# Softcap attention with two gated layers on one core: third key tile's scores in plain fp32, its sums partly on VectorE

## Chip, core and metric

The kernel runs on one core of a Trainium2 chip. The metric is the device time of one execution in microseconds; lower is better. Three runs of the kernel before gave 323.43, 324.13 and 324.26 us, the median is 324.13 us.

## What is computed

Attention over 2 batches, 12 heads, 448 positions and 64 channels per head, with scores capped by a tanh, then a gated layer with spatial mixing, then a gated layer with a convolution over positions. All in fp32. Cut to what the change touches:

```python
scale = 1.0 / np.sqrt(q.shape[-1])
scores = scale * np.matmul(q, k.transpose(0, 1, 3, 2))
scores = cap * np.tanh(scores / cap)
scores = scores - np.max(scores, axis=-1, keepdims=True)
attn = np.exp(scores)
attn = attn / (np.sum(attn, axis=-1, keepdims=True) + 1e-09)
out = np.matmul(attn, v)
...
h = gelu(x @ w_in)          # x: the heads side by side, 768 wide; h: 1024 wide
# then normalisation, a 448 x 448 mix, w_out; then x @ w2_in, a convolution, a gate, w2_out
```

## The kernel before

The heads go in pairs: 12 pairs `N` (6 per batch), the two heads of a pair on SBUF partitions 0 to 63 and 64 to 127. Scores are computed transposed, keys on PSUM partitions and the 448 queries along the free axis, in key tiles of 128, 128, 128 and 64 keys. The exponentials need no maximum, since the cap bounds them.

Two halves of a pair are two steps `R = 2 * N + half` of the loop at L619. `scores(N, 0)` computes key tiles 0 and 1 of both heads into the PSUM tile `sc` (one buffer), ScalarE takes a tanh (L412) and an exponential (L421) of it into `raw`. `scores(N, 1)` does the same for tile 2 (128 keys) and the last 64 keys. A product in full fp32 accuracy is made in one of two ways. In the first, VectorE splits an operand into a rounded `fp32r` part and a remainder, and TensorE runs three fp32r matmuls (high by high, high by low, low by high); key tiles 0 to 2 go this way, with `prep_q` and `prep_k` making the splits, `prep_q` for the next pair, with the factor `qscale = 1 / (8 * cap)` put on it. In the second, TensorE multiplies plain fp32 operands, which the trace shows as two records per matmul; the last 64 keys go this way, as four matmuls of 64 x 64 weights, one per quarter of the array, from `klast` (the keys times `qscale`) and the raw queries `qr`.

The sum over the keys and the product with the values are TensorE work as well. `value(N, g)` multiplies key tile g of `raw` by the values `V` (plain fp32, four column groups of 32 side by side), into the PSUM tile `pv`. For the softmax's denominator, VectorE adds tile 0 and tile 1 of `raw` into `held` (the tile `sm`, L472), and `values` multiplies it by a block of ones (`su`, four matmuls); after the second half, eight more such matmuls sum key tile 2 and the last keys. `norm` then copies sums and products out of PSUM (`E`, L542, ScalarE), sends the sums through DRAM to spread them over partitions (`ss`, `d`, `rb`, GpSimd's queue), and VectorE multiplies and splits the result into `X`, the input of the next stage. The last pair does this on TensorE instead (`norm_pe`, with the matmuls `pv<-E,sel`).

Beside this, the weights of the next stage are read (`f`, one piece of 128 x 512 float64 words at the steps in `WIN`), and turned into fp32r pairs `WI` by `decode_half`: `hd` (a cast), a shift and an or into `f`, a cast to `WI`, and a subtraction for the remainder, the last three on VectorE, the first on VectorE in the early pairs and on ScalarE from `R = 11` on. `FILL` puts pieces of the next stage's first products (`mo`, `fi`) between the attention's matmuls at the steps R = 15, 19, 23 and after the last scores at 24, 25 and 26.

Two things set the order. TensorE's attention matmuls go through `ordered`, which chains each to the one before, so they stand in the order of the code. `pin` chains instructions of ScalarE, VectorE and the SP queue in the same way where it is used; the rest is placed by the compiler's scheduler, which estimates times and issues what it takes to be ready. On the chip every engine then works through its fixed list.

`values(N, ...)` lags behind `scores`: on TensorE, the values and sums of pair N - 1 stand between the scores of pair N. A round, in what follows, is the stretch from the first score matmul of a pair to that of the next pair.

Of the kernel before, what the change touches and what calls it, by code (L numbers as in the profile page):

```python
# [19 lines left out]
P = 128  # L20
# [18 lines left out]
TAKEN = 4  # L39

# [13 lines left out]
def stages(  # L54
# [228 lines left out]
    def attention(att, psa):  # L283
# [5 lines left out]
        Kt = [att.tile([P, 2, ST], F32R, name=f"K{i}") for i in range(2)]  # L289
        kraw = [att.tile([P, S], F32, name=f"kr{i}") for i in range(2)]  # L290
        klast = [att.tile([P, D], F32, name=f"kl{i}") for i in range(2)]
        qraw = {}

        def load(n):
            b, p = divmod(n, NPAIR)
            qr = att.tile([P, S], F32, tag="qr", name="qr", bufs=3)
            kr = kraw[n % 2]
            k0 = 0 if n else K0
            for h in range(2):
                r = slice(h * D, (h + 1) * D)  # L300
                dma = sync if n or h else nc.scalar.dma_start
                dma(qr[r], qT[b, p, r, h])
                if k0:
# [15 lines left out]
        def prep_q(n):  # L319
            qr, _ = qraw[n]  # L320
            q = Qt[n] = att.tile([P, 2, S], F32R, tag="Q", name="Q", bufs=2)
            if n == 0:

                lasta[0] = A.activation(q[:, 0], qr, AF.Copy)
                lastv[0] = V.tensor_tensor(out=q[:, 1], in0=qr, in1=f(q[:, 0]), op=ALU.subtract)
                return
            V.tensor_scalar(out=q[:, 0], in0=qr, scalar1=qscale[:, 0:1], scalar2=None, op0=ALU.mult)
            lastv[0] = V.scalar_tensor_tensor(
                out=q[:, 1], in0=qr, scalar=qscale[:, 0:1], in1=f(q[:, 0]),
                op0=ALU.mult, op1=ALU.subtract,  # L330
            )

        def prep_k(n, c=slice(0, ST)):
            _, kr = qraw[n]
            K = Kt[n % 2]
            lastv[0] = split(kr[:, c], K[:, 0, c], K[:, 1, c])
            if c.stop < ST:
                return
            if n == 0:
                G.tensor_copy(klast[0], kr[:, ST:])  # L340
            else:
                V.tensor_scalar(
                    out=klast[n % 2], in0=kr[:, ST:], scalar1=qscale[:, 0:1], scalar2=None, op0=ALU.mult
                )
# [24 lines left out]
        with pin(lastv):  # L369
            prep_k(0, slice(0, K0))  # L370
        constants(att)
        creg = A.alloc_register("creg")
        with pin(lasta):
            A.reg_load(creg, capc[0:1].bitcast(mybir.dt.int32))

# [9 lines left out]
        with pin(lastv):  # L385
            prep_k(0, slice(K0, ST))
# [14 lines left out]
        def scores(N, half, then=None):  # L401
# [6 lines left out]
            sc = {"scale": qscale} if N == 0 else {}  # L408

            def soft(x, ps):  # L410
                with pin(lasta):
                    lasta[0] = A.activation(x, ps, AF.Tanh, **sc)  # L412
                if N == 1 and half:
                    with pin(lasta):
                        late.pop()()
                if half or N:
                    expo(x)
# [12 lines left out]
            for g in range(2 * half, 2 * half + 2):  # L430
# [4 lines left out]
                if g < 3:  # L435

                    for i, (j, l) in enumerate(((0, 0), (0, 1), (1, 0))):
                        for h in range(2):
                            r = slice(h * D, (h + 1) * D)
                            out, x = to[:, g * 2 + h, :S] if g < 2 else ps[:, h, :2], q[r, l]  # L440
                            if g == 2:
                                x = x.rearrange("p (i c) -> p i c", i=2)
                            ordered(out, lhsT=K[r, j, c], rhs=x, start=i == 0, stop=i == 2)
                else:

                    qr, _ = qraw.pop(N)
                    for h in range(2):
                        r = slice(h * D, (h + 1) * D)
                        for i in range(2):
                            ordered(  # L450
                                ps[i * D : (i + 1) * D, h, 2], lhsT=klast[N % 2][r],
# [14 lines left out]
            if half:  # L466
                soft(raw, ps)
            elif N:
# [31 lines left out]
        def values(N, half, done=False):  # L500
# [11 lines left out]
            for g in range(2 * half, 3 * half + 1):  # L512
                x = raw if half else held.pop(N)
                for t in range(4):
# [4 lines left out]
                        rhs=x[:, h, g - 2 + c if g == 2 else 2] if half else x[:, h, c * HS : (c + 1) * HS],  # L519
# [99 lines left out]
        for R in range(2 * NN + LAGS[1] + 1):  # L619
# [40 lines left out]
            if R in FILL:  # L660

                i, k0, k1 = FILL[R]
                if k0 == 0:
                    if i == 1:
                        free = psa.tile([P, 4, 512], F32, tag="sc", name="fi", bufs=1)
                    fill[i] = free[:, i, :S] if i % 2 else psm.tile([P, 512], F32, tag="mo", name="mo")[:, :S]
# [84 lines left out]
    def rest():  # L751
# [183 lines left out]
        with ExitStack() as s2, ExitStack() as last:  # L935
# [40 lines left out]
            def f_unit(b, m):  # L976
# [128 lines left out]
```

## Time and profile before

| | |
|---|---|
| median of three runs | 324.13 us |
| the profiled execution | 323.95 us |
| its span, first to last instruction | 322.1 us |
| TensorE busy in the span | 314.3 us (98%) |
| VectorE busy | 227.1 us (70%) |
| ScalarE busy | 207.0 us (64%) |
| attention | from the start to about 107 us of the span |

The profile is of one execution. A page gives the busy time of each engine and the chain of work that ended last; the timeline gives each engine's instructions in order of time, with the idle time before an instruction and what ended it in brackets. Starts of matmuls are good measures, their ends are modelled: how long a group of matmuls takes is read from its start to the start of the next group. Plain fp32 matmuls count twice in the timeline (x8 for four).

### The profile page before, as it was taken

What the parts mean: (1) busy time and instruction counts of PE and PEld (TensorE: products, weight loads), DVE (VectorE), ACT (ScalarE), POOL (GpSimd) and SP (SyncE); (2) the same over time, 40 slices, a digit from 0 to 9 for tenths busy, and PEclk for the clock granted to TensorE, in tenths of its full rate; (3) what the DMA queues carried; (4) which work ended last, traced back from release to release, by engine and by line L of the source; (5) the groups of instructions that cost most, each with busy time, mean ns of one, the idle gap of its engine ahead of it and who ended that gap; (6) DMA issues with size and microseconds to landing.
All of it is one profiled execution on the core that took longest, in us unless ns stands there. A gap on an engine that the chain in (4) does not pass through costs nothing.

```text
span 322.1 us, 6326 instructions
## 1 busy us (share of the span) xinstructions
PE 314.3 (98%) x2374; PEld 260.2 (81%) x2374; DVE 227.1 (70%) x474; ACT 207.0 (64%) x342; POOL 41.1 (13%) x76
## 2 busy tenths in 40 slices
PE   8999999999999999999999999999999999999992
PEld 6566666666677789988999999999999999999992
DVE  4557797699485999879995999979999997000000
ACT  4999999898963466646854745568867986111010
POOL 4000132241342060211112000000000000000000
PEclk9999999999999999999999999999999999999998
DMA  3477996855432253132124570012592301110111
GB/s 113 122 216 200 261 246 150 242 159 170 147 121 88 71 162 94 59 98 67 35 98 164 198 259 0 3 65 67 156 319 79 98 3 58 57 59 28 57 58 38
DMA packets 24526, 37.72 MB, mean 117 GB/s; under 512 B 7608, under 2 KB 22472, under 8 KB 24488
## 3 DMA queue, kind: packets, MB, share of 16 engines
q1 hardware_dynamic: 22552, 34.22, 34.3%
q0 software_dynamic: 1632, 2.61, 3.1%
q8 instruction: 20, 0.33, 0.4%
q10 hardware_dynamic: 304, 0.41, 0.4%
q14 instruction: 18, 0.15, 0.2%
HBM read 34.39 MB, written 2.79 MB: 115 GB/s over the span
## 4 chain that ended last, share of the span: by engine, by line
PE 95%; SPq 2%; DMA 1%; issue 0%; DVE 0%; ACT 0%; ACTq 0%
PE mo L114 18%; PE mo L112 18%; PE mo L113 18%; PE pv L395 16%; PE sc L395 9%; PE mo L798 3%; PE mo L799 3%; PE mo L800 3%; PE mo L395 3%; PE fi L395 2%; SPq L86 2%; DMA V<-in_vL_dram 1%; PE mo L845 1%; PE mo L844 1%; PE idle L395 0%
## 5 line engine op out<-in xcount | busy, mean ns | idle before, releaser
L112 PE MATMUL mo<-X,WI 128*128 128x448 f32 x120 | 43.5, 365 | 0.0
L114 PE MATMUL mo<-X,WI 128*128 128x448 f32 x120 | 43.5, 365 | 0.0
L113 PE MATMUL mo<-X,WI 128*128 128x448 f32 x120 | 43.5, 365 | 0.0
L421 ACT ACTIVATE raw<-raw 128x1344 f32<-128x1344 f32 (+2 forms) x25 | 36.4, 1461 | 0.7
L114 PE MATMUL mo<-HG,W 128*128 128x448 f32 x96 | 35.1, 365 | 0.0
L113 PE MATMUL mo<-HG,W 128*128 128x448 f32 x96 | 35.0, 365 | 0.0
L112 PE MATMUL mo<-HG,W 128*128 128x448 f32 x96 | 34.4, 365 | 0.0
L412 ACT ACTIVATE raw<-sc 128x1792 f32<-128x1792 f32 (+1 forms) x22 | 32.5, 1476 | 2.2 <-PE sc L395 2.0
L395 PE MATMUL pv<-raw,V 128*32 128x224 f32 x576 | 32.9, 358 | 0.2 <-DMA V<-in_vL_dram 0.2
L986 DVE TENSOR_SCALAR o<-mo 128x224 f32<-128x224 f32 x1 | 0.4, 392 | 44.8 <-ACT o L985 44.8
L989 ACT ACTIVATE o<-mo 128x448 f32<-128x448 f32 x11 | 5.8, 538 | 35.8 <-PE mo L114 35.8
L395 PEld LDWEIGHTS pv<-raw,V 128*32 128x32 f32 x576 | 19.0, 109 | 11.6 <-issue 5.8
L395 PE MATMUL sc<-Q,K 64*128 64x448 f32 x210 | 27.6, 385 | 0.5 <-ACT raw L412 0.4
L395 PEld LDWEIGHTS sc<-Q,K 64*128 64x128 f32 x210 | 17.9, 184 | 9.7 <-ACT raw L412 5.6
L112 PEld LDWEIGHTS mo<-X,WI 128*128 128x128 f32 x120 | 22.5, 188 | 1.9
L113 PEld LDWEIGHTS mo<-X,WI 128*128 128x128 f32 x120 | 22.5, 188 | 1.9
L114 PEld LDWEIGHTS mo<-X,WI 128*128 128x128 f32 x120 | 22.5, 188 | 1.9
L153 ACT ACTIVATE hs<-f 128x256 f16<-128x256 bf16 x36 | 16.4, 487 | 6.3 <-DMA f<-in_w_in_dram 6.0
L112 PEld LDWEIGHTS mo<-HG,W 128*128 128x128 f32 x96 | 18.0, 188 | 1.4
L114 PEld LDWEIGHTS mo<-HG,W 128*128 128x128 f32 x96 | 18.0, 188 | 1.4
L113 PEld LDWEIGHTS mo<-HG,W 128*128 128x128 f32 x96 | 18.0, 188 | 1.4
L168 DVE TENSOR_TENSOR WI<-f,WI 128x256 fp32r<-128x256 f32 (+1 forms) x36 | 18.2, 510 | 0.9 <-ACT WI L163 0.7
(159 smaller groups left out, 702.4 us busy)
## 6 DMA issues: line engine op xcount, KB each, us to landing
f<-in_w_out_dram SPq DMA_DIRECT2D x36, 255.8 KB, 2.7
f<-in_w_in_dram SPq DMA_DIRECT2D x12, 511.8 KB, 5.0
f<-in_w_in_dram SPq DMA_DIRECT2D x24, 255.8 KB, 3.3
qr<-in_qT_dram SPq DMA_DIRECT2D x23, 112.0 KB, 3.5
rb<-d POOLq DMA_DIRECT2D x22, 112.0 KB, 3.6
out_dram<-o SPq DMA_DIRECT2D x11, 224.0 KB, 1.9
V<-in_vL_dram SPq DMA_DIRECT2D x12, 192.0 KB, 4.0
kr<-in_kT_dram SPq DMA_DIRECT2D x11, 112.0 KB, 3.7
```

What stands on the lines that cost most here:

```text
L86: lasts[0] = nc.sync.dma_start(dst, src)
L112: matmul(ps, lhsT=whi, rhs=xhi, start=start, stop=False)
L113: matmul(ps, lhsT=whi, rhs=xlo, start=False, stop=False)
L114: matmul(ps, lhsT=wlo, rhs=xhi, start=False, stop=stop)
L153: A.activation(half, top, AF.Copy)
L168: V.tensor_tensor(out=lo, in0=f(low), in1=f(hi), op=ALU.subtract)
L395: lastm[0] = T.matmul(*args, **kw)
L412: lasta[0] = A.activation(x, ps, AF.Tanh, **sc)
L421: lasta[0] = A.activation(x, x, AF.Exp, scale=creg)
L798: T.matmul(ps, lhsT=xs(0, k), rhs=WI[1][:, 0, k], start=k == 0, stop=False)
L799: T.matmul(ps, lhsT=xs(0, k), rhs=WI[1][:, 1, k], start=False, stop=False)
L800: T.matmul(ps, lhsT=xs(1, k), rhs=WI[1][:, 0, k], start=False, stop=k == NK - 1)
```

## The change

1. Key tile 2 is no longer split. Its scores are plain fp32 in quarters, four matmuls of 64 keys by 64 channels with 448 columns each, from the raw keys and the raw queries, in place of six fp32r matmuls. `prep_k` splits 256 keys in place of 384, and `klast` is gone: the last 64 keys are read from `kr` as well, which gets three rotating buffers in place of two fixed ones.
2. The factor `qscale` moves from the operands to the tanh, as its scale (a register `qreg` on ScalarE; the first pair had it there already). `prep_q` becomes a plain split.
3. In the seven pairs of `ADD`, VectorE adds key tile 2 of `raw` into `held` after the second half's exponential. Those pairs have no sum matmuls after the first half; after the second, four matmuls sum `held` and four the last keys.
4. The fills at R = 15, 19 and 23 stand after the sums in place of before the values; at R = 24, both halves of the last pair's values come together, ahead of the fill of R = 25.
5. The last output tile is taken out of PSUM by one ScalarE instruction in place of one on ScalarE and one on VectorE.

```diff
+ADD = (1, 2, 3, 5, 7, 9, 10)
...
-            kr = kraw[n % 2]
+            kr = att.tile([P, S], F32, tag="kr", name="kr", bufs=3)
...
-            V.tensor_scalar(out=q[:, 0], in0=qr, scalar1=qscale[:, 0:1], scalar2=None, op0=ALU.mult)
-            lastv[0] = V.scalar_tensor_tensor(
-                out=q[:, 1], in0=qr, scalar=qscale[:, 0:1], in1=f(q[:, 0]),
-                op0=ALU.mult, op1=ALU.subtract,
-            )
+            lastv[0] = split(qr, q[:, 0], q[:, 1])
...
-            lastv[0] = split(kr[:, c], K[:, 0, c], K[:, 1, c])
...
+            lastv[0] = split(kr[:, :K0], K[:, 0], K[:, 1])
...
+            A.reg_load(qreg, qscale[0:1].bitcast(mybir.dt.int32))
...
-            sc = {"scale": qscale} if N == 0 else {}
+            sc = qreg if N else qscale
...
-                    lasta[0] = A.activation(x, ps, AF.Tanh, **sc)
+                    lasta[0] = A.activation(x, ps, AF.Tanh, scale=sc)
...
+                elif g == 2:
+                    qr, kr = qraw[N]
+                    x = qr.rearrange("p (i c) -> p i c", i=2)
+                    for h in range(2):
+                        r = slice(h * D, (h + 1) * D)
+                        for i in range(2):
+                            o, w = slice(i * D, (i + 1) * D), slice(K0 + i * D, K0 + (i + 1) * D)
+                            ordered(ps[o, h, :2], lhsT=kr[r, w], rhs=x[r], start=True, stop=True)
...
                 soft(raw, ps)
+                if N in ADD:
+                    x = held[N].rearrange("p h (i c) -> p h i c", i=2)
+                    V.tensor_tensor(out=x, in0=x, in1=raw[:, :, :2], op=ALU.add)
...
-            for g in range(2 * half, 3 * half + 1):
-                x = raw if half else held.pop(N)
+            for g in ((0, 3) if half else ()) if N in ADD else ((2, 3) if half else (0,)):
+                x = raw if g else held.pop(N)
...
+            if R in FILL and R >= 2 * NN:
+                units()
             tick()
             if R > 2 and done < 2 * NN and R - done >= LAGS[R >= LAGS[2]]:
                 values(*divmod(done, 2))
                 done += 1
+                if R == 2 * NN:
+                    values(*divmod(done, 2))
+                    done += 1
+            if R in FILL and R < 2 * NN:
+                units()
...
-                    A.activation(o[:, :HS], ps[:, :HS], AF.Copy, scale=0.5)
-                    V.tensor_scalar(out=o[:, HS:], in0=ps[:, HS:], scalar1=0.5, scalar2=None, op0=ALU.mult)
+                    A.activation(o, ps, AF.Copy, scale=0.5)
```

The order of VectorE around rounds 2 and 3, before. `sm_258` belongs to pair 1, `sm_336` to pair 2, `Q_338` and `K1` to pair 3, `f64_282` is the first piece of weights:

```order
L472 TENSOR_TENSOR sm_258<-raw_239 128x896
L327 TENSOR_SCALAR Q_338<-qr_230,one_72 128x448
L106 CAST K1_88<-kr1_90 128x384
L342 TENSOR_SCALAR kl1_92<-kr1_90,one_72 128x64
L328 SCALAR_TENSOR_TENSOR Q_338<-qr_230,one_72,Q_338 128x448
L109 TENSOR_TENSOR K1_88<-kr1_90,K1_88 128x384
L155 CAST hd0_137<-f64_282 128x512
L159 SCALAR_TENSOR_TENSOR f64_282<-f64_282,hd0_137 128x512
L165 CAST WI0_76<-f64_282 128x512
L168 TENSOR_TENSOR WI0_76<-f64_282,WI0_76 128x512
L472 TENSOR_TENSOR sm_336<-raw_321 128x896
```

The same place of VectorE's list after the change. `sm_253` belongs to pair 1, `raw_279` is that pair's second half, `sm_330` belongs to pair 2:

```order
L467 TENSOR_TENSOR sm_253<-raw_234 128x896
L108 CAST Q_332<-qr_224 128x448
L108 CAST K1_88<-kr_225 128x256
L111 TENSOR_TENSOR Q_332<-qr_224,Q_332 128x448
L111 TENSOR_TENSOR K1_88<-kr_225,K1_88 128x256
L157 CAST hd0_135<-f64_276 128x512
L161 SCALAR_TENSOR_TENSOR f64_276<-f64_276,hd0_135 128x512
L167 CAST WI0_76<-f64_276 128x512
L170 TENSOR_TENSOR WI0_76<-f64_276,WI0_76 128x512
L462 TENSOR_TENSOR sm_253<-sm_253,raw_279 128x896
L467 TENSOR_TENSOR sm_330<-raw_315 128x896
```

The new addition (L462) of pair 1 stands behind the four instructions of the first piece of weights, where pair 2's `sm` stood; pair 2's follows it. The additions of pairs 2 and 3 stand in the same way behind the second and third piece.

TensorE in round 2, before. `pv` rows with `raw_285`, `sm_258` are pair 1's, `sc` rows pair 2's:

```order
L395 MATMUL sc_320<-Q_276,K0_87 128x448 x12
L395 MATMUL pv_161<-raw_239,V_168 32x224 x16
L395 MATMUL pv_161<-sm_258,ones2_145 32x224 x4
L395 MATMUL sc_366<-Q_276,K0_87 128x2x224 x6
L395 MATMUL sc_366<-qr_162,kl0_91 64x224 x4
L395 MATMUL pv_161<-raw_285,vlast_110 64x224 x4
L395 MATMUL pv_161<-raw_285,V_168 32x224 x8
L395 MATMUL pv_161<-raw_285,ones2_145 32x224 x4
L395 MATMUL pv_161<-raw_285,ones0_143 32x224
```

And after the change:

```order
L382 MATMUL sc_314<-Q_271,K0_87 128x448 x12
L382 MATMUL pv_157<-raw_234,V_165 32x224 x16
L382 MATMUL sc_355<-qr_158,kr_159 64x2x224 x4
L382 MATMUL sc_355<-qr_158,kr_159 64x224 x4
L382 MATMUL pv_157<-raw_279,vlast_108 64x224 x4
L382 MATMUL pv_157<-raw_279,V_165 32x224 x8
L382 MATMUL pv_157<-sm_253,ones2_144 32x224 x4
L382 MATMUL pv_157<-raw_279,ones0_142 32x224
```

The sum over `sm` of pair 1 moved from ahead of the second half's scores to the end of the round, and now reads what VectorE's new addition wrote; the second half's scores follow the first values at once.

TensorE where the scores have ended, before:

```order
L395 MATMUL fi_1326<-X_75,WI0_76 128x448 x18
L395 MATMUL pv_161<-raw_1223,V_1118 32x224 x16
L395 MATMUL pv_161<-sm_1238,ones2_145 32x224 x4
L395 MATMUL mo_1382<-X_75,WI0_76 128x448 x18
L395 MATMUL pv_161<-raw_1269,vlast_110 64x224 x4
L395 MATMUL pv_161<-raw_1269,V_1118 32x224 x8
L395 MATMUL pv_161<-raw_1269,ones2_145 32x224 x4
```

And after the change, where the fill of R = 23 (`mo`, x6) comes just ahead:

```order
L382 MATMUL mo_872<-X_75,WI0_76 128x448 x6
L382 MATMUL fi_1274<-X_75,WI0_76 128x448 x18
L382 MATMUL pv_157<-raw_1179,V_1080 32x224 x16
L382 MATMUL pv_157<-sm_1194,ones2_144 32x224 x4
L382 MATMUL pv_157<-raw_1221,vlast_108 64x224 x4
L382 MATMUL pv_157<-raw_1221,V_1080 32x224 x8
L382 MATMUL pv_157<-raw_1221,ones2_144 32x224 x4
```

The last pair's values and sums are one group there, with the 18 `mo` matmuls behind it.

## Rows read from the trace of the kernel before

**Rows 1.** The page: the span, and the chain that ended last, by engine.

```profile
span 322.1 us, 6326 instructions
...
PE 95%; SPq 2%; DMA 1%; issue 0%; DVE 0%; ACT 0%; ACTq 0%
```

**Rows 2.** Timeline of TensorE, round 2: start us, us, engine, instruction.

```profile
17.89 1.49 PE L395 MATMUL sc<-Q,K 64*128 64x448 f32 x12
19.31 1.76 PE L395 MATMUL pv<-raw,V 128*32 128x224 f32 x32
20.85 0.60 PE L395 MATMUL pv<-sm,ones 128*32 128x224 f32 x8
21.37 0.88 PE L395 MATMUL sc<-Q,K 64*128 64x448 f32 x6
22.18 0.61 PE L395 MATMUL sc<-qr,kl 64*64 64x224 f32 x8
22.61 0.56 PE L395 MATMUL pv<-raw,vlast 64*64 64x224 f32 x8
23.10 0.98 PE L395 MATMUL pv<-raw,V 128*32 128x224 f32 x16
23.88 0.96 PE L395 MATMUL pv<-raw,ones 128*32 128x224 f32 x16
24.77 1.49 PE L395 MATMUL sc<-Q,K 64*128 64x448 f32 x12
```

**Rows 3.** Timeline of ScalarE, rounds 2, 3 and 8.

```profile
18.33 1.33 ACT L421 ACTIVATE raw<-raw 128x1344 f32<-128x1344 f32 x1
19.55 1.67 ACT L412 ACTIVATE raw<-sc 128x1792 f32<-128x1792 f32 x1
...
26.29 1.67 ACT L412 ACTIVATE raw<-sc 128x1792 f32<-128x1792 f32 x1 [0.16 <-PE sc L395]
...
68.99 0.79 ACT L153 ACTIVATE hd<-f 128x512 f16<-128x512 bf16 x1
```

**Rows 4.** Timeline of VectorE, rounds 2 to 5; in brackets idle time, and its releaser.

```profile
23.20 0.52 DVE L155 CAST hd<-f 128x512 f16<-128x512 bf16 x1 [2.15 <-DMA f<-in_w_in_dram]
...
25.77 1.08 DVE L472 TENSOR_TENSOR sm<-raw 128x896 f32<-128x896 f32 x1
...
30.32 0.51 DVE L155 CAST hd<-f 128x512 f16<-128x512 bf16 x1 [1.59 <-DMA f<-in_w_in_dram]
...
32.82 1.08 DVE L472 TENSOR_TENSOR sm<-raw 128x896 f32<-128x896 f32 x1
...
37.84 0.54 DVE L155 CAST hd<-f 128x512 f16<-128x512 bf16 x1 [1.93 <-DMA f<-in_w_in_dram]
...
40.27 1.08 DVE L472 TENSOR_TENSOR sm<-raw 128x896 f32<-128x896 f32 x1
```

**Rows 5.** Timeline of the SP queue: the issue of the first piece of weights.

```profile
18.71 0.43 SPq L86 DMA_DIRECT2D f<-in_w_in_dram  x1
```

**Rows 6.** Timeline of TensorE, round 7, the fill of R = 15.

```profile
56.70 0.61 PE L395 MATMUL sc<-qr,kl 64*64 64x224 f32 x8
57.24 1.48 PE L395 MATMUL mo<-X,WI 128*128 128x448 f32 x6
58.65 0.61 PE L395 MATMUL pv<-raw,vlast 64*64 64x224 f32 x8
```

**Rows 7.** Timeline of ScalarE and VectorE, the last output tiles.

```profile
306.64 0.54 ACT L989 ACTIVATE o<-mo 128x448 f32<-128x448 f32 x1 [4.32 <-PE mo L114]
...
316.37 0.36 ACT L985 ACTIVATE o<-mo 128x224 f32<-128x224 f32 x1 [4.32 <-PE mo L114]
...
316.75 0.39 DVE L986 TENSOR_SCALAR o<-mo 128x224 f32<-128x224 f32 x1 [44.85 <-ACT o L985]
```

**Rows 8.** Windows at the span's end: us, busy by engine, granted clock, DMA.

```profile
318.00:320.00 2.00, 0.00 (x0) 0.00 (x0) 0.00 (x0) 0.00 (x0) 0.00 (x0) 0.91 0.35 123
320.00:322.00 2.00, 0.00 (x0) 0.00 (x0) 0.00 (x0) 0.00 (x0) 0.00 (x0) 0.50 0.02 8
```

More of the change, by code (lines that the diff above doesn't have):

```diff
@@ L283, in attention @@
     def attention(att, psa):
-        Kt = [att.tile([P, 2, ST], F32R, name=f"K{i}") for i in range(2)]
-        kraw = [att.tile([P, S], F32, name=f"kr{i}") for i in range(2)]
-        klast = [att.tile([P, D], F32, name=f"kl{i}") for i in range(2)]
+        Kt = [att.tile([P, 2, K0], F32R, name=f"K{i}") for i in range(2)]
         qraw = {}
@@ L326, in prep_q, with prep_k @@
                 return
-            V.tensor_scalar(out=q[:, 0], in0=qr, scalar1=qscale[:, 0:1], scalar2=None, op0=ALU.mult)
-            lastv[0] = V.scalar_tensor_tensor(
-                out=q[:, 1], in0=qr, scalar=qscale[:, 0:1], in1=f(q[:, 0]),
-                op0=ALU.mult, op1=ALU.subtract,
-            )
-        def prep_k(n, c=slice(0, ST)):
+            lastv[0] = split(qr, q[:, 0], q[:, 1])
+        def prep_k(n):
             _, kr = qraw[n]
             K = Kt[n % 2]
-            lastv[0] = split(kr[:, c], K[:, 0, c], K[:, 1, c])
[L337 to L344, printed above, removed]
+            lastv[0] = split(kr[:, :K0], K[:, 0], K[:, 1])
         G.dma_start(capt, cap.partition_broadcast(P))
@@ L369, in attention @@
         with pin(lastv):
-            prep_k(0, slice(0, K0))
+            prep_k(0)
         constants(att)
-        creg = A.alloc_register("creg")
+        creg, qreg = A.alloc_register("creg"), A.alloc_register("qreg")
         with pin(lasta):
             A.reg_load(creg, capc[0:1].bitcast(mybir.dt.int32))
+            A.reg_load(qreg, qscale[0:1].bitcast(mybir.dt.int32))
         ones = [att.tile([P, 32], F32, name=f"ones{i}") for i in range(3)]
@@ L384, in attention @@
             G.memset(sel[t * 32 : t * 32 + 1, t], 1.0)
-        with pin(lastv):
-            prep_k(0, slice(K0, ST))
         raws, acc, held, pairs = {}, {}, {}, []
@@ L434, in scores @@
                 c = slice(g * P, (g + 1) * P)
-                if g < 3:
+                if g < 2:
                     for i, (j, l) in enumerate(((0, 0), (0, 1), (1, 0))):
@@ L439, in scores @@
                             r = slice(h * D, (h + 1) * D)
[L440 to L443, printed above, removed]
+                            ordered(to[:, g * 2 + h, :S], lhsT=K[r, j, c], rhs=q[r, l], start=i == 0, stop=i == 2)
+                elif g == 2:
[6 more added lines that the diff above has]
+                            ordered(ps[o, h, :2], lhsT=kr[r, w], rhs=x[r], start=True, stop=True)
                 else:
-                    qr, _ = qraw.pop(N)
+                    qr, kr = qraw.pop(N)
                     for h in range(2):
@@ L450, in scores @@
                             ordered(
-                                ps[i * D : (i + 1) * D, h, 2], lhsT=klast[N % 2][r],
+                                ps[i * D : (i + 1) * D, h, 2], lhsT=kr[r, ST:],
                                 rhs=qr[r, i * HS : (i + 1) * HS], start=True, stop=True,
@@ L518, in values @@
                         lhsT=ones[2 if g < 3 else c],
-                        rhs=x[:, h, g - 2 + c if g == 2 else 2] if half else x[:, h, c * HS : (c + 1) * HS],
+                        rhs=x[:, h, c if g == 2 else 2] if g else x[:, h, c * HS : (c + 1) * HS],
                         start=False, stop=g == 3, tile_position=(0, t * 32), skip_group_check=True,
@@ L659, in attention, with units @@
                         prep_k(N + 1)
-            if R in FILL:
+            def units():
                 i, k0, k1 = FILL[R]
@@ L664, in attention @@
                     if i == 1:
-                        free = psa.tile([P, 4, 512], F32, tag="sc", name="fi", bufs=1)
-                    fill[i] = free[:, i, :S] if i % 2 else psm.tile([P, 512], F32, tag="mo", name="mo")[:, :S]
+                        fill[-1] = psa.tile([P, 4, 512], F32, tag="sc", name="fi", bufs=1)
+                    fill[i] = fill[-1][:, i, :S] if i % 2 else psm.tile([P, 512], F32, tag="mo", name="mo")[:, :S]
                 for k in range(k0, k1):
```

## Prediction

> **What bounds the kernel now.** I read the page first: TensorE's own work makes 95% of the chain that ended last [rows 1], so a microsecond taken from TensorE's list counts in full, and so does one in which TensorE is made to wait. Then the timeline of TensorE over one round of the attention [rows 2]: its groups follow each other without idle time, and the starts give the price of each. The 12 score matmuls take 19.31 - 17.89 = 1.42 us, the first values 1.54, the sum over `sm` 0.52, the third key tile's scores 0.81, the last keys' 0.43, the values of the last keys 0.49, of tile 2 0.78, the last sums 0.89; in all 6.88 us. Rounds 3 to 6 repeat it within 0.02 us. Then ScalarE, which is nearly as full: what matters is when its tanh gives the one score buffer back [rows 3]. And VectorE, which is not full, but takes its list in order and three times sits idle for a piece of weights [rows 4]; the reader should see what stands behind those idle times.
>
> **The change part by part.**
>
> *Third key tile in plain fp32.* Four quarter matmuls of 448 columns replace six fp32r ones, 0.81 us. The trace has the same quarters with 224 columns at 0.43 us and 0.49 us [rows 2]; twice the dearer is 0.98. From below: the first values are 32 records in eight slots of four, 1.54 / 8 = 0.193 us for 224 columns; a fp32 matmul of 448 columns makes two records of double length, 4 x 0.193 = 0.77. I take 0.77, since the groups of 0.43 and 0.49 hold a change of shape which doubling would count twice. That is -0.04 us a pair; the upper end is +0.17.
>
> *Sums.* In seven pairs the 0.52 us of the sum over `sm` go from TensorE. They don't all come off: the second half's scores then follow the first values at once, into the buffer which the tanh of the first half is still reading. In a steady round the tanh starts 26.29 - 24.77 = 1.52 us after the round and takes 1.67 [rows 3], so these scores start at 3.25 us (with 0.06 for the handover), not at 1.42 + 1.54 = 2.96. Before they start at 3.48. So a round with the addition saves 0.23 + 0.04 = 0.27 us, where nothing else waits. Of seven, four lie behind round 5 (rounds 6, 8, 10 and 11).
>
> *Fills.* A fill between scores and values costs 1.41 us, and makes the group ahead of it 0.54 in place of 0.43 [rows 6, 2]: 1.52. Behind the sums it needs no change between fp32 and fp32r of its own. From 12 and 6 score matmuls (1.42 and 0.81) a step of two 64-row matmuls costs 0.20 and the change 0.20 [rows 2]; six fill matmuls are then 1.22, at the most 1.41. Gain 0.11 to 0.30 each, with what the group behind it loses up to 0.35; I take 0.3, three times: -0.9.
>
> *Last pair's group, output.* One alternation between fp32 and fp32r fewer at the end: 0.20 in, and 0.52 - 0.39 = 0.13 out, -0.33. The spread matmuls (`pv<-E,sel`) now stand 18 `mo` matmuls behind the last sum, 18 x 0.20 + 0.20 = 3.8 us, an estimate by the same steps, which I take to cover ScalarE's copy and VectorE's reciprocal; if it doesn't, TensorE waits there for the rest, a few tenths. The output tile: 316.37 to 317.14 is 0.77 us, since VectorE's half waits for ScalarE's; one instruction of 448 columns takes 0.54 [rows 7]: -0.23.
>
> *Splits and the tanh's scale.* VectorE drops the scaling and a third of the key split; off the path, at nothing. The register scale is what the exponential has already; at nothing.
>
> *ScalarE.* In the late rounds it also casts weights, 0.79 us each [rows 3]. Rounds with a shorter path on TensorE let it fall behind, and the tanh starts late; I charge 0.5 in all (0 to 1.6, twice that cast).
>
> *The new wait.* The sum over `sm` now reads what VectorE's addition wrote. The addition of pair 1 could run when the exponential is done, 18.33 + 1.33 = 19.66 us [rows 3]. But in VectorE's list it stands behind the first piece of weights: `hd`, which waits for its DMA until 23.20, and three more, in the place where pair 2's `sm` stood, 25.77 [rows 4]. The piece was issued at 18.71 [rows 5], and the SP queue's list ahead of it is the same after the change. So the addition ends at 25.77 + 1.08 = 26.85. TensorE is there earlier: the tanh of round 2 ends at 19.55 + 1.67 = 21.22, and 0.06 + 0.77 + 0.43 + 0.49 + 0.78 behind it, at 23.75, it wants the sums: 3.1 us idle. Behind the waiting sum in TensorE's list stand the other sums and round 3's scores, for those ScalarE's tanh, and for the end of the sums its copy of `pv`; the whole round moves. Round 3 begins at 26.90 + 0.89 = 27.79, not 24.77. It wants the sums 3.25 + 0.77 + 0.43 + 0.49 + 0.78 = 5.72 us later, 33.51; the addition of pair 2 stands behind the second piece, in the place of 32.82, and ends at 33.90: 0.45 idle. Round 4 begins at 34.84 and wants pair 3's sum at 40.56; that stands behind the third piece, 37.84, in the place of 40.27, and ends at 41.35: 0.85 idle. Round 5 begins at 42.29, where before it began at 24.77 + 2 x 6.88 = 38.53: **3.8 us late**. The third piece alone fixes this: without any wait, round 4 would want its sum at about 36.97 (rounds 3 and 4 beginning at 24.64 and 31.25), so the addition is 4.4 us late whatever the first two do. From there on no addition should be late: pair 4 has none, in round 6 it has some 0.4 us to spare, later rounds have no piece that VectorE waits for ahead of it.
>
> By the Trainium skill (TensorE: Matmul & The Clock Gate, Part 2, the step that loads the stationary operand) only weight loads are pulled ahead, and matmuls stay in program order; no run here shows one passing another. By that rule nothing fills the wait; if TensorE could take the 1.42 us of the next scores ahead of the sum, the result would be some 1.4 us better, 324.3.
>
> *Sum.* Late by 3.8 at round 5. Behind it: four rounds of 0.27 (-1.08), three pairs without the addition of 0.04 (-0.12), fills -0.9, end -0.33, output -0.23, ScalarE +0.5: -2.16. Together **+1.6 us**: the profiled execution's 323.95 becomes 325.55, and since the median of the runs, 324.13, is 0.18 above it, the median becomes **325.7**.
>
> **The rivals.**
>
> *The additions come in time.* Then rounds 2 to 4 save 0.13, 0.27 and 0.27, and the change ends at 324.13 - 0.67 - 2.16 = **321.3**, faster. It decides on the pieces of weights: the first would have to land by 23.7 - 1.08 - 2.57 (from `hd` to the place of `sm`) = 20.05, 1.3 us after its issue in place of 4.5, and the third 4.4 us sooner than in the trace. For it: the trace is one execution, and DMA landings vary. Against it: all three pieces made VectorE wait [rows 4], with the same queue ahead of them. Chance 0.12.
>
> *The clock falls in the wait.* At the end of the span, with the last matmul done by 316.37 [rows 7], the granted clock means 0.91 in 318 to 320 and 0.50, the 1.2 GHz level, in 320 to 322 [rows 8]; so TensorE without work loses its clock. If the 3.1 us of round 2 do that, some 1 to 4 us of matmul work take twice as long until the clock is back, of which the waits of rounds 3 and 4, 1.3 us, swallow a part. I take +1.0 net: **326.7** (325.7 to 328.4). Chance 0.15. The Trainium skill (same page, Part 1, on what is actually happening) calls the throttled state the default, released by activity; by that the fall is possible in any long enough wait, and rows 8 agree that it happens.
>
> *The quarters are dear.* At 0.98 us in place of 0.77, the nine rounds which no wait covers pay 0.21 more each: **327.6**. For it, the 0.49 us of one such group; against it, the 0.43 of the other. Chance 0.08.
>
> *The change doesn't do what it says:* the lists show the sums gone from the seven pairs, so this has no chance of its own.
>
> **How the numbers follow.** The forecast has 0.65: 325.7, with its own range from 324.3 (fills at 0.35, no loss on ScalarE, pieces half a microsecond sooner) to 327.2 (fills at 0.11, ScalarE at 1.6). With the rivals, the range that should hold the time 8 times in 10 is 322.5 to 328.0; the additions in time lie below it. About 0.3%, 1.0 us, is what a measurement of this kernel can tell from no change. Faster by more: the first rival and a thin tail of the forecast, 0.15. Within: a lower fifth of the whole, 0.20. Slower: 0.65.
>
> **What would show it.** TensorE idle for about 3 us near 23.7 with VectorE's L462 as releaser, and about 0.5 and 0.9 us near 33.5 and 40.5; `hd` idle for its DMA as before, L462 right behind the weights' subtraction. Round 5 beginning near 42.3. Rounds with the addition, behind it, of 6.6 us; second scores 3.25 us after a round's start, their group 0.77. Fills of 1.2 us between sums and scores. The forecast is wrong if L462 runs soon after 19.7, or if TensorE gains more than 2.2 us behind round 5; a clock below 1.00 between 24 and 32 us would be the second rival.

## The result: slower, and where the time went

The changed kernel takes 326.49 us (median; 326.07 to 328.67) where the kernel before takes 324.26 beside it: a ratio of 1.0076, 95% interval 1.0047 to 1.0105. That is slower by 2.2 us between the medians, 2.5 by the ratio; the forecast was 1.6. Ratios leave out executions that lie over 1.5% above the fastest of their kernel: none of the changed kernel, and of the runs told below one of a3_from_pair5 (331.47), two of e1_late_adds (326.97, 327.83) and one of g1_sums_behind (326.99). The profiled execution took 326.43 us with a span of 324.6, that is 2.48 us more than the one of before.

The page after, the rows that answer to [rows 1]:

```profile
span 324.6 us, 6272 instructions
...
PE 78%; ACT 6%; SPq 5%; DVE 4%; DMA 3%; issue 2%; DVEq 0%; ACTq 0%
```

TensorE's share of the chain fell from 95% to 78%. What came into it is ScalarE (6%), VectorE (4%) and more of the SP queue and of DMA: somewhere TensorE waited for them. The timeline of TensorE from round 2 to the start of round 5 says where (compare [rows 2]):

```profile
18.15 1.49 PE L382 MATMUL sc<-Q,K 64*128 64x448 f32 x12
...
21.53 1.46 PE L382 MATMUL sc<-qr,kr 64*64 64x448 f32 x16 [0.20 <-ACT raw L399]
...
26.51 0.59 PE L382 MATMUL pv<-sm,ones 128*32 128x224 f32 x8 [2.23 <-DVE sm L462]
...
27.43 2.61 PE L382 MATMUL sc<-Q,K 64*128 64x448 f32 x12
29.97 2.11 PE L382 MATMUL pv<-raw,V 128*32 128x224 f32 x32
32.01 1.36 PE L382 MATMUL sc<-qr,kr 64*64 64x448 f32 x16
33.20 0.56 PE L382 MATMUL pv<-raw,vlast 64*64 64x224 f32 x8
...
35.35 1.49 PE L382 MATMUL sc<-Q,K 64*128 64x448 f32 x12
...
42.05 1.49 PE L382 MATMUL sc<-Q,K 64*128 64x448 f32 x12
```

The sum over `sm` waits 2.23 us for VectorE's new addition, L462. Behind the wait the same work is slow: round 3's twelve scores take 29.97 - 27.43 = 2.54 us where they took 1.42, its first values 2.04 where they took 1.54. Rounds 3 and 4 have no wait for VectorE. Round 5 begins at 42.05; in the trace before it began at 38.52:

```profile
38.52 1.49 PE L395 MATMUL sc<-Q,K 64*128 64x448 f32 x12
```

VectorE's timeline shows what L462 stood behind (compare [rows 4]):

```profile
22.92 0.47 DVE L157 CAST hd<-f 128x512 f16<-128x512 bf16 x1 [2.48 <-DMA f<-in_w_in_dram]
...
25.37 1.08 DVE L462 TENSOR_TENSOR sm<-sm,raw 128x896 f32<-128x896 f32 x1
...
28.83 0.46 DVE L157 CAST hd<-f 128x512 f16<-128x512 bf16 x1
...
36.41 0.47 DVE L157 CAST hd<-f 128x512 f16<-128x512 bf16 x1 [0.28 <-DMA f<-in_w_in_dram]
...
38.76 1.07 DVE L462 TENSOR_TENSOR sm<-sm,raw 128x896 f32<-128x896 f32 x1
```

The first piece of weights makes VectorE wait as before, and the addition comes right behind it. The second piece, in a round that now begins later, no longer makes VectorE wait, the third for 0.28 us only, and TensorE waits for neither.

The windows (us, TensorE busy, granted clock, DMA share, GB/s) show why the work behind the wait is slow:

```profile
24.00:26.00 2.00, 0.28 (x8) 1.00 0.37 122
26.00:28.00 2.00, 1.49 (x20) 0.83 0.97 303
28.00:30.00 2.00, 2.00 (x15) 0.50 0.91 243
30.00:32.00 2.00, 2.00 (x34) 0.82 0.84 188
32.00:34.00 2.00, 2.00 (x36) 1.00 1.16 241
```

After 0.28 us of work in 24 to 26, the granted clock falls to 0.50, the 1.2 GHz level, while TensorE is full; by 32 it is back.

Behind round 5 the change gains: rounds 5 to 11 take 52.09 us in place of 53.20, the end up to the next stage's products 16.58 in place of 16.91 (with the 1.10 us of the spread matmuls, `pv<-E,sel`, which before stood among those products).

### The profile page after: what moved, and what is told of

Same layout as the page of the kernel before. It is cut to its first block, busy times and chain, and to the rows that moved or that the text cites. A ratio compares the mean times of both kernels' runs of the same rounds, so it can differ in the third digit from the quotient of the medians.

```text
span 324.6 us, 6272 instructions
## 1 busy us (share of the span) xinstructions
PE 313.5 (97%) x2342; PEld 260.3 (80%) x2342; DVE 227.2 (70%) x467; ACT 206.3 (64%) x342; POOL 38.4 (12%) x75
## 4 chain that ended last, share of the span: by engine, by line
PE 78%; ACT 6%; SPq 5%; DVE 4%; DMA 3%; issue 2%; DVEq 0%; ACTq 0%
PE mo L115 17%; PE mo L116 17%; PE mo L114 17%; PE pv L382 7%; PE sc L382 6%; SPq L88 5%; ACT raw L399 4%; PE mo L802 3%; PE mo L800 3%; PE mo L801 3%; PE fi L382 2%; DMA kr<-in_kT_dram 2%; PE mo L382 2%; DMA f<-in_w_in_dram 1%; ACT raw L408 1%
## 5 line engine op out<-in xcount | busy, mean ns | idle before, releaser
L114 PE MATMUL mo<-HG,W 128*128 128x448 f32 x96 | 34.4, 365 | 0.0
L116 PE MATMUL mo<-HG,W 128*128 128x448 f32 x96 | 34.4, 365 | 0.0
L115 PE MATMUL mo<-HG,W 128*128 128x448 f32 x96 | 34.4, 365 | 0.0
L467 DVE TENSOR_TENSOR sm<-raw 128x896 f32<-128x896 f32 x12 | 13.1, 1091 | 11.1 <-ACT raw L408 11.1
L382 PE MATMUL sc<-qr,kr 64*64 64x448 f32 (+1 forms) x192 | 17.1, 454 | 1.3 <-ACT raw L399 1.0
L382 PE MATMUL sc<-Q,K 64*128 64x448 f32 x138 | 18.3, 399 | 0.0
```

Of the source, the lines that this page charges most:

```text
L114: matmul(ps, lhsT=whi, rhs=xhi, start=start, stop=False)
L115: matmul(ps, lhsT=whi, rhs=xlo, start=False, stop=False)
L116: matmul(ps, lhsT=wlo, rhs=xhi, start=False, stop=stop)
L382: lastm[0] = T.matmul(*args, **kw)
L467: sms[N] = [V.tensor_tensor(out=held[N], in0=raw[:, 0:2], in1=raw[:, 2:4], op=ALU.add)]
```

## The experiments

Each ratio is to the kernel before, run beside the kernel on the same chip; it had medians of 324.08 to 324.44 us there. Medians and ranges count every execution.

| run | median us (range) | ratio, 95% interval |
|---|---|---|
| the change | 326.49 (326.07 to 328.67) | 1.0076 (1.0047 to 1.0105) |
| a4_ahead | 323.73 (322.46 to 325.77) | 0.9981 (0.9962 to 1.0000) |
| a1_not_pair1 | 325.18 (324.23 to 328.30) | 1.0043 (1.0018 to 1.0069) |
| a3_from_pair5 | 326.90 (325.59 to 331.47) | 1.0075 (1.0048 to 1.0103) |
| b1_warm | 325.25 (324.80 to 327.94) | 1.0042 (1.0024 to 1.0060) |
| c1_all_ahead | 323.06 (322.26 to 324.99) | 0.9951 (0.9926 to 0.9976) |
| c2_no_add | 324.25 (322.71 to 325.44) | 0.9985 (0.9957 to 1.0012) |
| c3_from_pair7 | 322.57 (321.92 to 324.50) | 0.9940 (0.9915 to 0.9965) |
| d1_fills_end | 323.78 (322.79 to 324.43) | 0.9967 (0.9942 to 0.9991) |
| e1_late_adds | 323.46 (321.92 to 327.83) | 0.9944 (0.9923 to 0.9965) |
| f1_plus_pair1 | 326.54 (325.51 to 328.71) | 1.0067 (1.0041 to 1.0093) |
| f2_plus_warm | 325.35 (324.54 to 329.18) | 1.0045 (1.0021 to 1.0069) |
| g1_sums_behind | 322.64 (321.85 to 326.99) | 0.9950 (0.9934 to 0.9967) |

### The additions ahead of the weights: a4_ahead

```diff
+        pair = now[0] // 4 if now[0] < 16 else None
...
-            with pin(lasta), pin(lastv):
+            with pin(lasta), pin(lastv), pin(adds.get(pair, [None])):
...
-                    V.tensor_tensor(out=x, in0=x, in1=raw[:, :, :2], op=ALU.add)
+                    adds[N] = [V.tensor_tensor(out=x, in0=x, in1=raw[:, :, :2], op=ALU.add)]
```

> The changed kernel, with the first three pieces of weights put behind the additions of pairs 1, 2 and 3 in VectorE's list. Theory: TensorE's 2.23 us wait in round 2 for the addition of pair 1, and the fall of its clock behind it (about 1.6 us in rounds 2 and 3), are the whole loss; both go. Round 2 begins near 18.15, rounds 2 to 4 take 6.6 to 6.75, round 5 begins near 38.2 in place of 42.05: 322.6 us, faster than both kernels. Rival (the loss sits in the additions' own cost on VectorE, in the startup or behind round 5): no less than 324.5.

The order alone gives back 0.0095 of the time, 3.1 us. Pair 1's addition now runs at 20.86, ahead of the first piece, and rounds 2, 3 and 4 begin at 18.00, 24.82 and 31.50 with no wait for it; round 5 begins at 38.18, as the theory had it. But the median is 1.1 us over the 322.6 expected, since part of the loss turns up two rounds later. VectorE's timeline, then TensorE's:

```profile
20.86 1.08 DVE L463 TENSOR_TENSOR sm<-sm,raw 128x896 f32<-128x896 f32 x1
...
49.39 0.23 DVE L558 TENSOR_SCALAR ss<-ss,one 128x14 f32<-128x14 f32 x1 [1.45 <-DMA ss<-E]
...
38.18 1.49 PE L383 MATMUL sc<-Q,K 64*128 64x448 f32 x12
...
41.55 0.59 PE L383 MATMUL pv<-sm,ones 128*32 128x224 f32 x8 [0.16 <-DVE sm L468]
...
45.40 1.50 PE L383 MATMUL sc<-Q,K 64*128 64x448 f32 x12
...
52.16 0.58 PE L383 MATMUL pv<-sm,ones 128*32 128x224 f32 x8 [0.76 <-DVE sm L463]
```

Round 5 takes 7.22 us, round 6 7.66. In round 5 it is pair 4's *first* sum that is late: the third piece of weights now landed at 38.10, ahead of it. In round 6 it is pair 5's addition, behind the add on `ss`, the sums of the softmax, for whose transfer VectorE waited 1.45 us.

### Additions taken away from the front: a1_not_pair1, a3_from_pair5

```diff
-ADD = (1, 2, 3, 5, 7, 9, 10)
+ADD = (2, 3, 5, 7, 9, 10)    # a1_not_pair1
+ADD = (5, 7, 9, 10)          # a3_from_pair5
```

> The changed kernel, pair 1 without the addition (its sums on TensorE again). If the addition of pair 1 alone makes the loss: rounds 2 to 4 take 6.84, 6.65 and 6.65, 322.8 us. If the next addition takes over, as the prediction had it for each piece by itself (pair 2's stands behind the second piece, wanted at about 30.7, ready between 32.2 by the trace of after and 33.9 by that of before): a wait of 1.5 to 3.2 us in round 3 and a clock that falls behind it, 325 to 327 us.

> The changed kernel, pairs 1, 2 and 3 without the addition. Theory: no wait and full clock in rounds 2 to 4, each 6.84; round 5 begins near 38.7: 323.1 us, that is the gains behind round 5 (about 1.5 us with the fills and the end) against a start that is 0.26 us later. Rival (the rest of the change loses time too): 324.3 or more.

In a1_not_pair1 the wait moves on, as its second case said, but it is shorter than the 1.5 to 3.2 us expected, and in the profiled execution the clock stays at 1.00 behind it. TensorE:

```profile
31.81 0.59 PE L382 MATMUL pv<-sm,ones 128*32 128x224 f32 x8 [0.80 <-DVE sm L462]
...
40.14 0.59 PE L382 MATMUL pv<-sm,ones 128*32 128x224 f32 x8 [1.43 <-DVE sm L462]
...
41.03 1.49 PE L382 MATMUL sc<-Q,K 64*128 64x448 f32 x12
```

Pair 2's addition is 0.80 us late, pair 3's 1.43, behind the second and third piece. Round 5 begins at 41.03, only 1.02 us sooner than in the changed kernel.

a3_from_pair5 is no better than the change: in its time it came out on the rival's side, but not for the rival's reason. Rounds 2 to 4 are as the theory has them (18.16, 24.99, 31.84, and round 5 at 38.66), and then TensorE waits in round 6, and its clock falls there. TensorE, VectorE and windows:

```profile
53.55 0.59 PE L382 MATMUL pv<-sm,ones 128*32 128x224 f32 x8 [2.06 <-DVE sm L462]
...
54.44 2.23 PE L382 MATMUL sc<-Q,K 64*128 64x448 f32 x12
...
50.80 0.23 DVE L557 TENSOR_SCALAR ss<-ss,one 128x14 f32<-128x14 f32 x1 [4.21 <-DMA ss<-E]
...
52.41 1.08 DVE L462 TENSOR_TENSOR sm<-sm,raw 128x896 f32<-128x896 f32 x1
...
52.00:54.00 2.00, 0.46 (x12) 1.00 0.55 166
54.00:56.00 2.00, 2.00 (x22) 0.73 0.53 143
56.00:58.00 2.00, 2.00 (x20) 0.50 1.03 371
```

Here the instruction ahead of the addition waits for no weights, but for the softmax sums of pairs 2 and 3 (`ss`), which GpSimd's queue spreads over partitions. In the changed kernel this does no harm: round 6 begins 3.4 us later there, and `ss` is in place without a wait. So the loss is not the addition of pair 1 as such. VectorE works through its list in order, and each of its waits for a transfer holds up the first addition behind it that TensorE comes for in time.

### No early additions, none at all, and the order alone: c3_from_pair7, c2_no_add, d1_fills_end

```diff
+ADD = (7, 9, 10)    # c3_from_pair7
+ADD = ()            # c2_no_add
```

d1_fills_end is the kernel before with parts 4 and 5 of the change and nothing of parts 1 to 3:

```diff
-            if R in FILL:
+            def units():
...
+            if R in FILL and R >= 2 * NN:
+                units()
...
+                if R == 2 * NN:
+                    values(*divmod(done, 2))
+                    done += 1
+            if R in FILL and R < 2 * NN:
+                units()
...
+                    A.activation(o, ps, AF.Copy, scale=0.5)
```

> The changed kernel with the additions of pairs 7, 9 and 10 alone, the three whose rounds have no early piece of weights ahead of them. If an addition is worth what rounds 8 and 10 of the trace after show (0.18 us each): 0.5 us under c2_no_add, 322.9 by the rows, 321.7 by the prediction's terms. If the wait only moves on to the first addition that is left, as from pair 1 to pair 2 in a1_not_pair1 and to pair 5 in a3_from_pair5: a wait of about 2 us in round 8 and a lower clock behind it, 325 to 327.

> The changed kernel without any addition on VectorE: its sums all on TensorE, the rest as changed. By the prediction's terms for the rest (quarters -0.04 a pair, fills -0.9, end -0.33, output -0.23) 322.2. By the rows of the trace after (fills of 1.41 us, a gain of 0.11 each; end -0.33; the output's gain not seen; a start that is 0.26 us later) 323.4. No wait of TensorE for VectorE in either. Rival (the quarters or the tanh's scale cost time): 324.5 or more.

> The kernel before with the changes of order alone: fills behind the sums, the last pair's groups together, the last output tile by one ScalarE instruction. By the prediction's terms -0.9 - 0.33 - 0.23: 322.6 us. By the rows of the trace after -0.33 - 0.33: 323.4. Its start shows whether the first scores at half pace until about 6.7 us belong to the change (here 0.96 us for the first six matmuls, as in the trace before) or to the execution (1.35 to 1.49).

c3_from_pair7 is 1.9 us faster than the kernel before: the additions that TensorE does not wait for seem to pay, 0.0045 or 1.5 us between c2 and c3 for three, where 0.5 were expected (the intervals overlap). The traces show less: rounds 8 and 10 take 6.68 us in place of c2's 6.82, round 11 8.41 in place of 8.37. c3's profiled execution, 323.85, is 1.3 us over its median, and waits at two places that no addition has to do with:

```profile
42.41 0.59 PE L382 MATMUL pv<-sm,ones 128*32 128x224 f32 x8 [1.11 <-DVE sm L467]
...
56.96 0.58 PE L382 MATMUL pv<-sm,ones 128*32 128x224 f32 x8 [0.68 <-DVE sm L467]
```

c2_no_add has the same two (0.49 and 1.22 us), where none was expected. These are the first sums of pairs 4 and 6, behind the third piece of weights and behind `ss`. In the kernel before the same order holds, and pair 4's ended at 40.27 + 1.08 = 41.35 [rows 4], when TensorE wanted it at 38.52 + 2.96 = 41.48: in time by 0.13 us. So even without additions a faster TensorE meets VectorE's list. c2_no_add, 0.9985 with an interval that includes 1, cannot be told from the kernel before; its 324.25 us lies nearer to its rival's 324.5 than to the 323.4 by the rows, and these two waits, 1.7 us in its profiled execution, are more than that difference.

d1_fills_end gains 0.0033, 1.1 us, between the rows' 0.7 and the prediction's 1.46; the interval, 0.3 to 1.9 us, allows both. A fill is 1.41 us long, in the changed kernel and here (here 59.55 to 60.96):

```profile
59.55 1.49 PE L395 MATMUL mo<-X,WI 128*128 128x448 f32 x6
60.96 1.29 PE L395 MATMUL sc<-Q,K 64*128 64x448 f32 x10
```

Rounds 7, 9 and 11 take 8.30, 8.41 and 8.32 us in place of 8.57, 8.57 and 8.55: -0.66 for the three fills.

### The clock by itself: b1_warm, f1_plus_pair1, f2_plus_warm

```diff
+            if N == 1 and half:
+                for _ in range(10):
+                    ordered(idle, lhsT=wz[:, :P], rhs=wz, start=True, stop=True)
```

This is b1_warm against the change, and f2_plus_warm against f1_plus_pair1. The latter is the kernel of e1_late_adds, below, with pair 1 in `ADD` as well.

> The changed kernel, with ten matmuls of 448 columns that nothing reads in TensorE's list ahead of pair 1's sum, in the stretch in which it waits. The wait for the addition stays. Theory: the granted clock stays at 1.00 from 24 to 34 us, round 3's first scores take 1.42 and not 2.54, and 1.6 us come back: 324.9 us. Rival (the clock costs nothing, because the next waits, for ScalarE's tanh or for the additions of pairs 2 and 3, swallow what it gives back): round 5 begins near 42 as before, 326.3 us.

> The kernel of e1_late_adds with the addition of pair 1 in its place behind the first piece of weights, and nothing else early: this one instruction alone. Theory: 2.2 us of waiting in round 2 and 1.2 to 1.6 of a lower clock in rounds 2 and 3 (0.50 to 0.85 granted), which nothing later gives back: 3.4 to 3.8 us over e1. Rival (a late start of round 4 only uses up slack that later waits would cost anyway): at most 1 us over e1.

> The kernel of f1_plus_pair1, with ten matmuls that nothing reads ahead of pair 1's sum, as in b1_warm. Theory: the wait stays and the clock too (1.00), 1.2 us of f1's loss come back: 2.2 to 2.4 us over e1. Rival (the clock's share is given back later anyway, by the shorter waits behind it): the same as f1 within 0.3 us.

In b1_warm the granted clock is 1.00 from 24 to 34. Round 2 lasts 9.17 us, so the wait is there, filled with matmuls; round 3 takes 6.71 in place of the change's 7.92:

```profile
24.07 2.29 PE L382 MATMUL idle<-wz 128*128 128x448 f32 x10
26.30 0.59 PE L382 MATMUL pv<-sm,ones 128*32 128x224 f32 x8
...
27.19 1.50 PE L382 MATMUL sc<-Q,K 64*128 64x448 f32 x12
...
33.90 1.49 PE L382 MATMUL sc<-Q,K 64*128 64x448 f32 x12
...
40.90 1.49 PE L382 MATMUL sc<-Q,K 64*128 64x448 f32 x12
```

Of the 1.2 us that round 3 wins, round 4 gives 0.3 back (7.00 in place of 6.70): pair 3's addition is late again, behind the third piece. Round 5 begins 1.15 us sooner, and the time is 1.1 us lower by the ratios (1.0042 against 1.0076; the intervals overlap), under the 1.6 expected.

f1_plus_pair1 and f2_plus_warm point the same way with nothing else early: one addition of pair 1 makes 1.0067 of e1's 0.9944, 4.0 us (3.1 between the medians; 3.4 to 3.8 expected), and the ten matmuls bring back 0.0022, 0.7 us (the intervals overlap), where 1.2 were expected. In their profiled executions the clock's share is larger. Timeline and windows of f1_plus_pair1:

```profile
26.74 0.97 PE L383 MATMUL pv<-sm,ones 128*32 128x224 f32 x8 [2.88 <-DVE sm L463]
...
28.39 2.61 PE L383 MATMUL sc<-Q,K 64*128 64x448 f32 x12
...
26.00:28.00 2.00, 1.26 (x16) 0.50 1.00 288
28.00:30.00 2.00, 2.00 (x16) 0.50 0.97 255
```

Its round 3 takes 8.68 us, that of f2_plus_warm 6.83. But this execution of f1 is the slowest of its six, 328.71. The mean granted clock of each execution is a sign of how often it falls; only the profiled ones show it. It is below 0.993 in three of five executions of the change, four of six of a3_from_pair5, three of twelve of a1_not_pair1, four of six of f1, three of seven of e1, one of twelve of f2 and of g1, and one of 99 of the kernel before; in none of a4, b1, c1, c2, c3 and d1, in whose traces TensorE is idle for no more than 1.3 us for VectorE. The two executions of the change with the clock kept took 326.07 and 326.49, the three others 326.43, 327.56 and 328.67. Two are few, but b1_warm, with the clock kept in all twelve by the same sign, is slower than the kernel before as well (1.0024 at the least): the wait alone makes the change slower, and the clock comes on top where it falls.

### Every addition and first sum ahead of the waits: c1_all_ahead, e1_late_adds, g1_sums_behind

```diff
+                if N == 4:
+                    adds[3] = sms[4]
...
-                with pin(lastv):
+                with pin(lastv), pin(adds[5] if N == 3 else [None]):              # c1_all_ahead
+                with pin(lastv), pin(sms[6] if N == 3 else [None]):               # e1_late_adds
+                with pin(lastv), pin(adds[N + 2] if N in (3, 5, 7) else [None]):  # g1_sums_behind
```

c1 and g1 have all seven additions and the order of a4_ahead; e1 has those of pairs 7, 9 and 10. The pins hold the third piece of weights behind pair 4's first sum, and the add on `ss` behind an addition or a first sum.

> The kernel of run a4_ahead, with two more orders on VectorE: the third piece of weights also behind pair 4's first sum, and the sums that come back from DRAM for pairs 2 and 3 (a wait for GpSimd's transfer) behind the addition of pair 5. In a4_ahead round 5 took 7.22 us and round 6 7.66, with TensorE waiting 0.16 us for pair 4's first sum and 0.76 for the addition of pair 5, both behind such an instruction. Theory (every addition that loses time stands behind a VectorE instruction that waits for a transfer): rounds 5 and 6 take 6.84 and 6.68, and the median is 1.3 us under a4_ahead: 322.4. Rival (a TensorE that is earlier meets the next late thing: ScalarE's tanh, or the addition of pair 7): 323.5 or more.

> The kernel of c3_from_pair7 (additions of pairs 7, 9 and 10 alone), with pair 4's first sum ahead of the third piece of weights on VectorE, and pair 6's ahead of the sums that come back from DRAM, the two for which TensorE waited 1.11 and 0.68 us there. Theory (such waits are all that is left between the rows of a round and the time): rounds 5 and 7 take 6.84 and 8.3, no wait in rounds 2 to 11, 1.8 us under c3's profiled execution of 323.85: a median of 322.1 to 322.4. Rival (c3's other executions did not have those waits, its median lies 1.3 us under its profiled run): no change from c3's 322.6.

> The kernel of c1_all_ahead (all seven additions, early pieces of weights behind them), with the sums that come back from DRAM for pairs 4 to 7 also put behind the additions of pairs 7 and 9, as those for pairs 2 and 3 already were behind pair 5's. In the profiled execution of e1_late_adds pair 7's addition stood behind such a sum, which waited 6.12 us for its transfer, and TensorE waited 2.71 us in round 8 and lost its clock, while four of its seven executions took 321.92 to 323.46. Theory (what scatters is the landing of a transfer ahead of an addition): no execution over 324, a median of 322.3 to 322.9. Rival (the scatter of c1, 322.26 to 324.99, has another cause): the same scatter and 323.1.

c1_all_ahead has no wait of TensorE for VectorE left. Rounds 5 and 6 take 6.86 and 6.68 us, and the seven additions that cost 2.2 us in the change's order stand in a kernel that is 0.0049 faster than before. The median is 0.7 us over the expected 322.4.

e1_late_adds shows in one execution what scatters. VectorE, TensorE and a window:

```profile
66.03 0.23 DVE L560 TENSOR_SCALAR ss<-ss,one 128x14 f32<-128x14 f32 x1 [6.12 <-DMA ss<-E]
...
68.78 0.59 PE L383 MATMUL pv<-sm,ones 128*32 128x224 f32 x8 [2.71 <-DVE sm L463]
...
70.00:72.00 2.00, 2.00 (x12) 0.50 0.89 284
```

The rounds 5 to 7 are free of waits, as the theory had it, and pair 7's addition stands behind the next `ss`. That execution took 325.71; four others, 321.92 to 323.46. The last two took 326.97 and 327.83 at a mean clock of 0.991, where the profiled one has 0.992: probably the same event, but there is no trace of them. g1_sums_behind puts those behind the additions too. Its profiled execution, 321.88, has no such wait, its median is 322.64, as the theory had it; but one of its twelve, against the theory, took 326.99 and two 323.5 to 323.6, so that not all of the scatter is explained. c3, e1, c1 and g1 cannot be told apart; all four beat both kernels, the one before by 1.6 to 1.9 us on the ratios. d1_fills_end, which has none of parts 1 to 3, has 0.9967, with an interval that overlaps theirs: how much of the gain the quarters and the additions bring is not settled by these runs.

## Why the prediction was right, and which steps were not

| term of the sum | predicted us | in the profiled execution |
|---|---|---|
| round 5 begins late by | 3.8 | 3.53, of which 0.26 from the start |
| rounds 5 to 11 (sums, quarters, fills, ScalarE) | -1.60 | -1.11 |
| end | -0.33 | -0.33 |
| output | -0.23 | -0.24 |
| anything else | 0 | +0.63 |
| sum | +1.6 | +2.48 |

**The wait** was right in its place, releaser and order, and 2.23 us long in place of 3.1. TensorE wanted the sum at 24.28 and not at 23.75 (0.26 of it the start, the rest the groups ahead of the sum, 2.75 us in place of 2.47), and the addition ended at 26.45, not 26.85 (0.28 of it the piece's landing). The last of those groups is counted to its modelled end, 0.98 us, where the next group starts 0.78 behind it elsewhere; by starts alone TensorE lost 2.43 us. a4_ahead shows that its order is the cause.

**Rounds 3 and 4** were wrong in the change's own trace: predicted were further waits of 0.45 and 0.85 us, and there are none. In their place stands the slower clock, 1.2 us in round 3. The step that failed is the choice between forecast and second rival: the clock did fall, just behind the wait. Its price there, 1.0 net of what the next waits swallow, is what b1_warm measures (round 5 sooner by 1.15, 0.13 of it from its start). With that rival the prediction said 326.7. That the median is 326.49 does not confirm it: the median execution is one that kept its clock. The three that did not have a median of 327.56, the two that did lie 0.4 and 0.8 us over the forecast of 325.7; why they are slower than b1_warm's 325.25 is open.

**"The third piece alone fixes this"** holds where the clock stays: in b1_warm and a1_not_pair1 round 5 begins at 40.90 and 41.03, whether pair 1 has its addition or not, each behind pair 3's (38.87 + 1.08 and 39.00 + 1.08). It was mis-sized by the third addition, which ended near 40.0 in place of 41.35. In the changed kernel the slower clock made round 4 later than that, and hid it. Two errors, 1.3 us too much for the piece and nothing for the clock, nearly cancel: that round 5 came out 3.53 us late, near the 3.8 forecast, is in part luck.

**From round 6 on no addition is late** was true, but for a reason that the prediction did not see: the 3.5 us already lost. a3_from_pair5 takes them away, and pair 5's addition is 2.06 us late behind a wait for `ss`. The prediction looked for weights ahead of the additions only.

**Quarters** were right: their group and the last keys' take 33.20 - 32.01 = 1.19 us, predicted 0.77 + 0.43. The third rival is out. **Sums** save 0.18 to 0.21 a round, not 0.27: rounds with the addition take 6.68 to 6.69, since the group of the last keys' values takes 0.58 us there in place of 0.49. That goes with second scores that start late, behind ScalarE's tanh, not with the addition: round 3 has the addition and 0.48 (its scores come late enough not to wait), round 9 has none and 0.58. **Fills** were mis-sized: 1.41 us, the upper end, not 1.22; -0.66 for three in d1_fills_end, not -0.9. Groups of 18 take 3.77 to 3.88 us, so six 1.26 to 1.29, not 1.22; the fill of round 11, which further fills follow, takes 1.33, so some of the 1.41 seems to come with the change to the scores behind it, though both are fp32r. **ScalarE** costs what was charged: its tanh is 0.42 us late in round 11. **End and output** were right; the spread matmuls wait for nobody. What the output saved, 1.27 to 1.03 us from the start of the last matmul to the DMA, the landing took back: 4.92 us from its issue to the end of the span before, 5.22 after, and 4.34 to 5.37 in the other traces. The rest of the +0.63 is a wait of 0.24 us for ScalarE's `VN` at 170 us and 0.1 spread over the products.

**The rival that the additions come in time** is what a4_ahead makes of the kernel, and c1 and g1 fully: predicted 321.3, measured 323.06 and 322.64. Fills and sums, over-sized again, are 0.7 us of the difference in c1's trace (rounds 2 to 4 give 0.43, not 0.67, rounds 5 to 11 1.11, not 1.60). Its later start is 0.28, and from the first `fi` matmul to the last product it takes 224.54 us, where 224.19 were taken before and 223.76 to 224.33 in the other traces; why that differs is open.

## What to carry to other kernels

Work that is moved to an engine with time to spare still stands in that engine's list: before it is moved, look at what the instruction just ahead of it waits for, and pin that instruction behind it where it is a transfer that nobody needs soon. Where two engines are matched to a few tenths of a microsecond, as here, a gain on one turns up as a wait behind the next transfer, so take waits out by order, all along the list, not one by one. On TensorE a wait can cost more than its length: behind the 2.23 us of the change the clock fell, and round 3 took 1.2 us more.

## What the runs showed of the hardware

The clock fell in or just behind waits of 2.23 us (the change), 2.06 (a3), 2.71 (e1) and 2.88 (f1), to 0.50, and in the profiled a1_not_pair1 not at all behind waits of 0.80 and 1.43 (1.00 from 28 to 44 us). By the mean clock it does not fall in every execution of the same kernel: three of five of the change. The Trainium skill (TensorE: Matmul & The Clock Gate, Part 1) says that the number of matmuls at the low clock at a kernel's start varies from run to run; these executions vary in a like way behind a wait, in the middle of the kernel.

At the very start the record of the granted clock and the pace differ. The first score matmuls in the change's trace:

```profile
5.41 1.49 PE L382 MATMUL pv<-Q,K 64*128 64x448 f32 x6
6.70 0.84 PE L382 MATMUL sc<-Q,K 64*128 64x448 f32 x6
```

and in that of c2_no_add, which has the same instructions there:

```profile
5.44 0.95 PE L382 MATMUL pv<-Q,K 64*128 64x448 f32 x6
6.22 0.78 PE L382 MATMUL sc<-Q,K 64*128 64x448 f32 x6
```

Six matmuls take 1.29 us in one execution and 0.78 in the other, at a recorded clock of 1.00 in both. Why is open. d1_fills_end, with the first instructions of the kernel before, takes 1.26 where that kernel takes 0.79, so both kernels have both paces, and the later start of round 2 is the execution's, not the change's: that round begins between 17.61 and 18.26 us in these traces.
